# Attention and a feed-forward layer on one core: late weight conversion, sums of x and the hand-over put in other places

## The chip, the core and the metric

The kernel runs on one core of a Trainium2 chip. A core has engines with instruction streams of their own: TensorE (PE, the matrix products, with PEld for its weight loads), VectorE (DVE), ScalarE (ACT), GpSimd (POOL) and SyncE (SP), which here issues nearly all DMAs. Each works through its stream in order and waits on semaphores for the others. The metric is the device time of one execution in microseconds; lower is better.

## The reference

Two layers, the second on the first one's output. `f` gives a decay along the sequence, the weights arrive as 64-bit floats.

```python
B, H, S, D = 8, 8, 576, 64
scores = np.matmul(q, k.transpose(0, 1, 3, 2)) / np.sqrt(D)
cum = np.cumsum(np.log(np.clip(f, 0.0001, 1.0)), axis=-1)
scores = np.where(causal, -1e9, scores + cum[:, :, :, None] - cum[:, :, None, :])
...
x = softmax(scores) @ v                  # laid out as 4608 tokens x 512
h = x @ w_in                             # 512 x 2048
g = h * erf(softplus(h))
return g @ w_out                         # 2048 x 512
```

## The kernel before

**Attention** is a pipeline over t = 0 to 68 with 64 steps of work (NH = 64: 32 pairs of heads, each in two halves). For step t it issues scores(t), the reductions and exponentials, normalize(t-2), transposes(t-3), values(t-4) and store(t-5). `store` copies the outputs o from PSUM into a tile xo on DVE (L564, L567, L568) and writes it to the DRAM tensor xt_d from SP's queue (L570). From t = 64 on, the products of the first two feed-forward units run between the last steps.

**The weights** come as 64-bit floats and are turned on the chip into a high and a low part in float32r (a type that TensorE multiplies in one pass), written to DRAM as wi_d and wo_d. A pair of feature blocks (called a feature here, numbered 0 to 7) has four raw tiles. For each: `words` (three DVE operations, L351 to L353) and `joined` (two, L360 and L369), then for w_out `out_high` on ACT and `out_low` on POOL (L380), for w_in `combine` (sums on POOL, L388), `in_high` on ACT and `in_low` on POOL (L398). `schedule` lays them out as a list of steps; `due` says how many are issued by each t. In the feed-forward part, `middle` takes two more steps in every unit, one between the flushes (after flush 3) and one behind the rounding of the gates.

**The feed-forward part** takes tokens in six blocks v of 768 and features in nine visits: blocks 0 to 2 with features 0 to 4, blocks 0 to 2 with features 5 to 7, blocks 3 to 5 with all eight. A unit is one feature of one visit; there are 48: units 0 to 14 (visits of five), 15 to 23 (visits of three), 24 to 47 (visits of eight). Within a unit, x @ w_in is done in seven products of half blocks, P1 to P7, instead of eight. Their x operands, numbered 0 to 6 in the order of the products, are the blocks 11, 12, 21, 22 of x and the differences T1, T2, "12" (in place of block 12) and T4. Each operand becomes a tile xs with a high part (ACT, L136) and a low part (two POOL operations, L140). The differences (two operations each, L131) are made on DVE, for the first visit alone on POOL. Each of P1 to P7 is six matmuls: high by high, high by low, low by high, for two halves of the depth.

The products go to PSUM banks a, b, x, y; P2 adds to P1 in a, so P2 must wait until DVE has copied P1 (L186). All of a's to y's banks exist once. For unit u, `middle(u)` issues on PE the products with w_out in six groups of six (`down`, L234), on ACT softplus and erf of unit u+1 (L205, L207, with table loads), on DVE six flushes that add y to a sum in SBUF (L253, L255) and four gates (h times erf, L215) between them, then `round_gate`: gh on ACT (L222), gl on POOL (L223); then `prepare`, which takes an equal share of the next visit's `x_steps`. After that come `up(u+2, 0)`, P1, P6, P7, P5 with the copy and three additions on DVE (L182), `up(u+2, 1)`, P2, P4, P3 with two additions, and the load of the weights of unit u+4. y has four buffers, each of u, e, gh, gl six, a weight tile two.

Work is issued by hand in program order for PE, DVE, ACT and POOL; a position in the code is a position in the engine's stream.

## Time and profile before

| | |
|---|---|
| median of 3 runs | 1206.84 us (1206.11 to 1208.26) |
| the profiled execution | 1209.55 us |
| its span, from the first to the last instruction | 1207.7 us |
| granted clock of TensorE, mean | 0.964 |
| share of the span that PE, DVE, ACT, POOL are busy | 92%, 71%, 59%, 51% |
| read and written in HBM | 231.88 MB, 46.81 MB |

A row of the timeline gives start, length, engine, line, operation, output <- inputs, shapes and count; in brackets how long the engine idled ahead of it and what ended that. Equal instructions in a row are put together (x6). In the order listings further down a row is one instruction (x2: two alike), named by line, operation and tiles; a tile's number tells it from others of the name.

In the page's 40 slices the clock (PEclk) and PE's share dip in the same places, the end of attention and the visits after it:

```profile
PE   5999899999995698979999898989999999999998
PEclk7999999999998798989999999989999999999999
```

### The profile page before, as it was taken

How to read it: one execution, taken by the hardware profiler on the slowest of the kernel's cores; microseconds unless marked ns; L12 is line 12 of the kernel's file. 1: busy time of each engine (PE TensorE's matmuls, PEld its weight loads, DVE VectorE, ACT ScalarE, POOL GpSimd, SP SyncE). 2: the span in 40 equal slices, each digit the busy share in tenths (PEclk: the TensorE clock that was granted, in tenths of full speed). 3: DMA queues.
4: the chain of work that ended last, by engine and by line, in shares of the span. 5: the costliest groups of instructions: out<-in, count | busy, mean ns of one | idle time of the engine just before them, and what ended most of it. 6: DMA issues, size and time to landing. Idle time of an engine off the chain costs nothing. (4 is left out here: it accounts for less than half of the span.)

```text
span 1207.7 us, 21855 instructions
## 1 busy us (share of the span) xinstructions
PE 1113.5 (92%) x7552; PEld 971.2 (80%) x7552; DVE 857.3 (71%) x1964; ACT 713.6 (59%) x1540; POOL 619.7 (51%) x734
## 2 busy tenths in 40 slices
PE   5999899999995698979999898989999999999998
PEld 3888788887885587868888877777899989999997
DVE  6888789998985677776766666575766676665555
ACT  3787678887874154536566455454565556555553
POOL 1666657788754346447445554545444434442233
PEclk7999999999998798989999999989999999999999
DMA  8698998878856456937847676747455755566532
GB/s 300 210 316 306 341 340 279 254 272 298 294 192 225 158 180 247 316 120 254 312 157 252 235 257 223 262 182 245 183 192 209 262 183 187 188 204 232 192 131 87
DMA packets 75725, 280.11 MB, mean 232 GB/s; under 512 B 7904, under 2 KB 17120, under 8 KB 63328
## 3 DMA queue, kind: packets, MB, share of 16 engines
q1 hardware_dynamic: 75616, 278.72, 66.2%
q8 instruction: 60, 0.98, 0.3%
q14 instruction: 49, 0.40, 0.1%
HBM read 231.88 MB, written 46.81 MB: 231 GB/s over the span
## 5 line engine op out<-in xcount | busy, mean ns | idle before, releaser
L223 POOL TENSOR_TENSOR gl<-e,gh 128x384 fp32r<-128x384 f32 x192 | 234.5, 1250 | 454.5 <-PE y L234 370.3
L234 PE MATMUL y<-wo,gh 128*128 128x512 f32 x1152 | 357.5, 392 | 13.6 <-DMA wo<-wo_d 13.6
L234 PEld LDWEIGHTS y<-wo,gh 128*128 128x128 f32 x1152 | 217.0, 189 | 57.2 <-issue 13.7
L255 DVE TENSOR_TENSOR ys<-y,ys 128x512 f32<-128x512 f32 x252 | 174.2, 691 | 97.4 <-PE y L234 97.4
L234 PE MATMUL y<-wo,gl 128*128 128x512 f32 x576 | 225.8, 392 | 0.0
L516 POOL TENSOR_SCALAR pr<-pr,st 128x576 f32<-128x576 f32 (+4 forms) x320 | 164.5, 535 | 118.1 <-DVE st L512 74.2
L505 ACT ACTIVATE pr<-pr,st 128x576 f32<-128x576 f32 (+3 forms) x320 | 176.7, 557 | 3.5 <-DVE st L493 3.5
L176 PE MATMUL pha<-xs,wi 128*128 128x384 f32 x576 | 125.3, 352 | 41.4 <-DVE u L186 40.3
L493 DVE CUSTOM_DVE_ANT_0 pr<-s,c 128x576 f32<-128x576 f32 (+3 forms) x320 | 136.4, 487 | 28.7 <-PE s L475 20.8
L176 PEld LDWEIGHTS pha<-xs,wi 128*128 128x128 f32 x576 | 105.3, 195 | 51.3 <-DVE u L186 41.7
L222 ACT CAST gh<-e 128x384 fp32r<-128x384 f32 x192 | 93.9, 514 | 83.8 <-DVE e L215 83.3
L205 ACT ACTIVATE e<-pha 128x384 f32<-128x384 f32 x48 | 23.6, 492 | 191.4 <-PE pha L176 184.1
L470 PE MATMUL s<-k,q 64*128 64x320 f32 (+4 forms) x768 | 121.1, 428 | 14.4 <-DMA k<-in_k_dram 8.3
L176 PE MATMUL phy<-xs,wi 128*128 128x384 f32 x576 | 123.5, 346 | 4.8 <-POOL xs L140 4.7
L234 PEld LDWEIGHTS y<-wo,gl 128*128 128x128 f32 x576 | 108.6, 189 | 22.9
L176 PE MATMUL phx<-xs,wi 128*128 128x384 f32 x576 | 125.0, 352 | 1.1 <-POOL xs L140 1.1
L205 ACT ACTIVATE e<-u 128x384 f32<-128x384 f32 x144 | 75.0, 522 | 77.0 <-DVE u L182 73.9
L182 DVE TENSOR_TENSOR u<-phx,u 128x384 f32<-128x384 f32 x96 | 53.5, 558 | 93.9 <-PE phx L176 91.9
L470 PEld LDWEIGHTS s<-k,q 64*128 64x128 f32 x768 | 80.9, 196 | 45.1 <-issue 20.4
L537 ACT COPY pt<-t 128x512 f32<-128x512 f32 x128 | 73.6, 577 | 71.2 <-PE t L528 71.2
L555 PE MATMUL o<-pt,v 128*64 128x128 f32 (+1 forms) x1920 | 104.4, 262 | 12.2 <-DVE xo L564 6.5
L555 PEld LDWEIGHTS o<-pt,v 128*64 128x64 f32 x1920 | 95.6, 139 | 22.1 <-issue 6.3
(68 smaller groups left out, 1709.8 us busy)
## 6 DMA issues: line engine op xcount, KB each, us to landing
wi<-wi_d SPq DMA_DIRECT2D x48, 1792.0 KB, 7.4
wo<-wo_d SPq DMA_DIRECT2D x48, 1024.0 KB, 4.8
v<-in_vp_dram SPq DMA_DIRECT2D x32, 576.0 KB, 7.2
c<-cum_d SPq DMA_DIRECT2D x62, 288.0 KB, 5.7
r<-xt_d SPq DMA_DIRECT2D x36, 384.0 KB, 4.7
q<-in_q_dram SPq DMA_DIRECT2D x32, 320.0 KB, 5.7
k<-in_k_dram SPq DMA_DIRECT2D x32, 288.0 KB, 6.0
xt_d<-xo SPq DMA_DIRECT2D x32, 288.0 KB, 7.2
```

The source lines that it names most:

```text
L176: nc.tensor.matmul(out=ps, lhsT=wi[:, w, n, kd], rhs=xs[:, x, kd], start=not part and kd == 0 and i == 0, stop=kd == 1 and i == 2, skip_gr ...
L205: nc.scalar.activation(out=e_, in_=h[c], func=AF.Softplus)
L222: nc.scalar.copy(out=gh, in_=e_)
L223: nc.gpsimd.tensor_tensor(out=gl, in0=e_, in1=gh.bitcast(F32), op=ALU.subtract)
L234: nc.tensor.matmul(out=y, lhsT=x[:, cs], rhs=wo[:, i, w], start=i == 0 and n == 0, stop=i == 1 and n == 2)
L255: nc.vector.tensor_tensor(out=ys, in0=y, in1=ys, op=ALU.add)
L470: nc.tensor.matmul(out=s[j][:, at:at + k1 - k0], lhsT=q[h, PAD + START[i]:PAD + END[i]], rhs=k[h, k0:k1], start=i > 0, stop=k1 < END[i])
L493: nc.vector.tensor_tensor_reduce(out=to[:, ::-1] if j else to, in0=score, in1=decay_, scale=-0.125, scalar=BIG, op0=ALU.add, op1=ALU.min, ...
L505: nc.scalar.activation(out=seg, in_=seg, func=AF.Exp, bias=st[:, 0, j, m:m + 1], scale=-1.0, accum_out=st[:, 1, j, m:m + 1])
L516: nc.gpsimd.tensor_scalar(out=seg, in0=seg, scalar1=st[:, 2, j, m:m + 1], scalar2=1.0, op0=ALU.mult, op1=ALU.mult)
L537: nc.scalar.copy(out=pt[:, 512 * a:512 * a + 512], in_=b)
L555: nc.tensor.matmul(out=o[h, to:to + width], lhsT=v[:, ch, h], rhs=pt[:, at[j]:at[j] + width], start=n == 0, stop=n == len(parts) - 1, skip ...
```

## The change

PE's order stays. Five things move:

- Conversion in attention ends with feature 4. The steps of features 5 to 7 get places of their own beside units 0 to 12 (`beside_units`): place 0 is ahead of flush 0 (`words` on DVE; `out_low`, `combine`, `in_low` on POOL), place 1 between the two parts of `up` (`joined`), place 2 behind the rounding (`out_high`, `in_high`).
- The differences of x go to the same places (`combine` of the class): T1 to place 0 of a visit's first unit, T2 and "12" to place 1 of it, T4 to place 0 of the unit after the one with xs 4. For visits 1 to 3 POOL makes them, for visits 4 to 8 DVE.
- `SPLITS` says which operands are split in which unit of the visit ahead.
- At the end of attention, activation and gates of unit 0 come at the end of step 65 instead of its start; the last store of xt_d is issued from ACT's queue; the load of the weights of unit 3 comes behind the first two loads of wo.
- Two tiles share another tag, and ACT's xs tiles 3, 4, 6 of odd visits come from the pool that held 3, 4, 5.

```diff
@@
     RINGS = {"u": 6, "e": 6, "gh": 6, "gl": 6}
     PRODUCTS = [("P1", "a"), ("P6", "b"), ("P7", "x"), ("P5", "y"), ("P2", "a"), ("P4", "x"), ("P3", "y")]
     FIRST = 4
+    X = ["11", "T2", "12", "T1", "21", "T4", "22"]
+    SPLITS = {3: [[0, 3, 4, 6], [1, 2, 5]], 5: [[0, 4], [3, 6], [1, 2], [5]], 8: [[0], [4], [3], [6], [1], [2], [5]]}
     TILES = ["11", "21", "22", "12"]
 
     def __init__(self, tc, xt_d, out, xp, wp):
@@
             self.nc.sync.dma_start(out=r, in_=self.xt_d[2 * i * P:2 * (i + 1) * P, c:c + TB]
                                    .rearrange("(k p) t -> p k t", p=P))
 
+    def sub(self, k, name, kds=range(2)):
+        nc, raw = self.nc, self.raw
+        a, b = {"T1": ("12", "11"), "T2": ("22", "T1"), "12": ("22", "12"), "T4": ("21", "T2")}[name]
+        if name != "12" and (k, name) not in raw:
+            raw[k, name] = self.half(name, k)
+        for kd in kds:
+            (nc.vector if k > HALF else nc.gpsimd).tensor_tensor(
+                out=raw[k, name][:, kd], in0=raw[k, a][:, kd], in1=raw[k, b][:, kd], op=ALU.subtract)
+
+    def high(self, k, n):
+        pool, bufs = (self.xq, 3) if k % 2 and n in (3, 4, 6) else (self.xp, 10)
+        self.xs[k, n] = x = pool.tile([P, 2, 2, TB], F32R, name=f"xs{k}_{n}", tag="xs", bufs=bufs)
+        self.nc.scalar.copy(out=x[:, 0], in_=self.raw[k, self.X[n]])
+
+    def low(self, k, n, kds=range(2)):
+        x = self.xs[k, n]
+        for kd in kds:
+            self.nc.gpsimd.tensor_tensor(out=x[:, 1, kd], in0=self.raw[k, self.X[n]][:, kd],
+                                         in1=x[:, 0, kd].bitcast(F32), op=ALU.subtract)
+
     def x_steps(self, k):
 
...
         steps = []
...
+        for n in range(7):
+            for name in {0: ("T1", "T2", "12"), 5: ("T4",)}.get(n, ()):
+                steps += [(self.sub, k, name, [kd]) for kd in range(2)]
+            steps += [(self.high, k, n)] + [(self.low, k, n, [kd]) for kd in range(2)]
         return steps
 
     def load_wi(self, u):
@@
             row = v * NW + tb * P
             nc.sync.dma_start(out=self.out[row:row + P] if a == NU - 1 else self.part_d[v * NTB + tb], in_=ys)
 
+    def combine(self, u, between):
+
+        k, i, a = self.units[u]
+        if k + 1 < len(self.visits):
+            four = [4 in n for n in self.SPLITS[len(self.visits[k][1])]].index(True) + 1
+            names = ("T2", "12") if between else ("T1",)
+            for name in names if i == 0 else ("T4",) if i == four and not between else ():
+                self.sub(k + 1, name)
+
     def prepare(self, u):
 
         k, i, a = self.units[u]
-        n = len(self.visits[k][1])
-        if i == 0:
-            self.later = self.x_steps(k + 1)
-        if i < n - 1:
-            for _ in range(-(-len(self.later) // (n - 1 - i))):
-                self.later.pop(0)()
-        if i == n - 2:
-            self.load_x(k + 2)
+        splits = self.SPLITS[len(self.visits[k][1])]
+        if k + 1 < len(self.visits) and i < len(splits):
+            for n in splits[i]:
+                self.high(k + 1, n)
+                self.low(k + 1, n)
+            if i == len(splits) - 1:
+                self.load_x(k + 2)
 
     def middle(self, u, convert):
 
         more = u + 1 < self.n
         ys = [self.down(u, tb) for tb in range(NTB)]
+        convert(u, 0)
+        self.combine(u, False)
         if more:
             self.activate(u + 1)
-        order = [("f", 0), ("f", 1), ("g", 0), ("f", 2), ("g", 1), ("f", 3), ("c", 0), ("g", 2), ("f", 4), ("g", 3),
-                 ("f", 5)]
+        order = [("f", 0), ("f", 1), ("g", 0), ("f", 2), ("g", 1), ("f", 3), ("g", 2), ("f", 4), ("g", 3), ("f", 5)]
         for what, n in order:
             if what == "f":
                 self.flush(u, n, ys[n])
-            elif what == "c":
-                convert()
             elif more:
                 self.gate(u + 1, n)
         if more:
             for n in range(4):
                 self.round_gate(u + 1, n)
-            convert()
+            convert(u, 2)
             self.prepare(u)
         del self.wo[u], self.g[u]
         self.load_wo(u + 2)
@@
                 work[8 * b + n].append((call, a, *args))
         return [work[n] for n in range(8 * len(features) + 5)]
 
+    def convert(steps):
...
@@
                 nc.vector.tensor_copy(out=xo[:, 192:448], in_=o[:, :256])
                 nc.vector.tensor_copy(out=xo[:, :64], in_=o[:, 256:320])
                 b, pp = divmod(p, NP)
-                nc.sync.dma_start(out=xt_d[pp * P:(pp + 1) * P, b * S:(b + 1) * S], in_=xo)
+                queue = nc.sync if t < NH - 1 else nc.scalar
+                queue.dma_start(out=xt_d[pp * P:(pp + 1) * P, b * S:(b + 1) * S], in_=xo)
                 del vals[p]
 
         NH = B * H
 
-        fd = [wk.tile([P, S], F32, name=f"fd{j}", tag=f"pt{j}", bufs=1) for j in range(2)]
+        fd = [wk.tile([P, S], F32, name=f"fd{j}", tag=f"pr{j}") for j in range(2)]
         for j in range(2):
             nc.sync.dma_start(out=fd[j], in_=f[0, j].partition_broadcast(P))
         fr = wk.tile([B * H, S], F32, name="fr", tag="xo")
@@
         load(1)
         load_weight(0)
         load_weight(1)
-        work = schedule(range(NU))
+        work = schedule(range(NU1 + 1))[:8 * NU1 + 5]
+        work[-1] = [step for step in work[-1] if step[0] is in_low]
         for t in range(NH + 5):
             there = [0 <= t - n < NH for n in range(6)]
             p, half = divmod(t, 2)
@@
                 moe.up((t - NH) // 2, (t - NH) % 2)
                 if t == NH + 1:
                     moe.load_wi(2)
-                    moe.activate(0)
-                    for n in range(4):
-                        moe.gate(0, n)
-                        moe.round_gate(0, n)
-                if t == NH + 3:
-                    moe.load_wi(3)
             if there[2]:
                 normalize(t - 2)
             if there[5]:
@@
             if there[3]:
                 for a in range(1, len(BANKS[(t - 3) % 2])):
                     evacuate(t - 3, a)
-            due = 2 * t + 2 if t < 4 else 8 + (8 * NU1 - 3) * (t - 3) // (NH - 4) if t < NH else 8 * NU1 + 6 + t - NH
-            while 8 * NU + 5 - len(work) < due:
-                convert(work)
+            due = 2 * t + 2 if t < 4 else 8 + (8 * NU1 - 4) * (t - 3) // (NH - 4)
+            while work and 8 * NU1 + 5 - len(work) < due:
+                convert(work.pop(0))
             if t > X0 and moe.later:
-                moe.later.pop(0)()
+                convert([moe.later.pop(0)])
+            if t == NH + 1:
+                moe.activate(0)
+                for n in range(4):
+                    moe.gate(0, n)
+                    moe.round_gate(0, n)
             if t == NH - 1:
                 early.close()
                 moe.ep = moe_pools.enter_context(tc.tile_pool(name="ep", bufs=2, side="right"))
                 moe.ps_h = moe_pools.enter_context(tc.tile_pool(name="ps_h", bufs=1, space=PSUM, side="right"))
-        assert not moe.later and not pts and not held and not vals
+        assert not work and not moe.later and not pts and not held and not vals
 
     moe.wop = ctx.enter_context(tc.tile_pool(name="wop", bufs=1))
     moe.xq = ctx.enter_context(tc.tile_pool(name="xq", bufs=1))
@@
     moe.ps_y = ctx.enter_context(tc.tile_pool(name="ps_y", bufs=1, space=PSUM))
     moe.load_wo(0)
     moe.load_wo(1)
+    moe.load_wi(3)
     moe.load_x(1)
     moe.want_y(0)
+    work = beside_units()
     for u in range(moe.n):
-        moe.middle(u, lambda: convert(work))
+        moe.middle(u, lambda u, place: convert(work.pop((u, place), ())))
         if u + 2 < moe.n:
             moe.up(u + 2, 0)
+            convert(work.pop((u, 1), ()))
+            moe.combine(u, True)
             moe.up(u + 2, 1)
             moe.load_wi(u + 4)
     assert not work
```

How the streams change at three places. First, DVE between the flushes of unit 0 and those of unit 1, before (rT and r are the halves of x that the next visit needs, phX the banks, wtop a weight under conversion, ys the sums of y):

```order
L360 SCALAR_TENSOR_TENSOR wtop_5652<-wraw_5494,wtop_5652 128x512
L369 SCALAR_TENSOR_TENSOR wtop_5652<-wraw_5494,wtop_5652 128x512
L131 TENSOR_TENSOR rT_1_5686<-r_1_5576,r_1_5574 128x384 x2
L131 TENSOR_TENSOR rT_1_5689<-r_1_5578,rT_1_5686 128x384 x2
L131 TENSOR_TENSOR r_1_5576<-r_1_5578,r_1_5576 128x384 x2
L186 COPY u_2_5727<-pha_5699 128x384
L182 TENSOR_TENSOR u_2_5727<-phb_5706,u_2_5727 128x384
L182 TENSOR_TENSOR u_2_5728<-phx_5713,u_2_5727 128x384
L182 TENSOR_TENSOR u_2_5728<-phy_5720,u_2_5728 128x384
L182 TENSOR_TENSOR u_2_5733<-phx_5713,u_2_5727 128x384
L182 TENSOR_TENSOR u_2_5727<-phy_5720,u_2_5727 128x384
L255 TENSOR_TENSOR ys_0_5582<-y_0_5756,ys_0_5582 128x512
```

The same place after the change, from the first addition behind the copy of P1 on:

```order
L181 TENSOR_TENSOR u_2_5680<-phb_5659,u_2_5680 128x384
L181 TENSOR_TENSOR u_2_5681<-phx_5666,u_2_5680 128x384
L181 TENSOR_TENSOR u_2_5681<-phy_5673,u_2_5681 128x384
L366 SCALAR_TENSOR_TENSOR wtop_5591<-wraw_4959,wtop_5591 128x512
L375 SCALAR_TENSOR_TENSOR wa_5688<-wraw_4959,wtop_5591 128x2x256
L181 TENSOR_TENSOR u_2_5686<-phx_5666,u_2_5680 128x384
L181 TENSOR_TENSOR u_2_5680<-phy_5673,u_2_5680 128x384
L357 TENSOR_SCALAR wtop_5761<-wraw_5194 128x512
L358 TENSOR_SCALAR wtop_5761<-wtop_5761 128x512
L359 TENSOR_SCALAR wtop_5761<-wtop_5761 128x512
L254 TENSOR_TENSOR ys_0_5543<-y_0_5719,ys_0_5543 128x512
```

The six differences are gone from ahead of the copy (L186 before); the pair L366, L375 of `joined` stands between the additions of the two parts, and the three of `words` ahead of flush 0 (L254).

Second, DVE at the end of attention, before, from the last additions of unit 1's products to the first flush (xo is the tile for the last store):

```order
L182 TENSOR_TENSOR u_1_5451<-phx_5431,u_1_5445 128x384
L182 TENSOR_TENSOR u_1_5445<-phy_5438,u_1_5445 128x384
L564 COPY xo_5518<-o_5474 128x2x128
L351 TENSOR_SCALAR wtop_5540<-wraw_5413 128x512
L352 TENSOR_SCALAR wtop_5540<-wtop_5540 128x512
L353 TENSOR_SCALAR wtop_5540<-wtop_5540 128x512
L567 COPY xo_5518<-o_5520 128x256
L568 COPY xo_5518<-o_5520 128x64
L360 SCALAR_TENSOR_TENSOR wtop_5540<-wraw_5413,wtop_5540 128x512
L369 SCALAR_TENSOR_TENSOR wtop_5540<-wraw_5413,wtop_5540 128x512
L253 COPY ys_0_5582<-y_0_5588 128x512
```

and after:

```order
L181 TENSOR_TENSOR u_1_5431<-phx_5411,u_1_5425 128x384
L181 TENSOR_TENSOR u_1_5425<-phy_5418,u_1_5425 128x384
L585 COPY xo_5492<-o_5454 128x2x128
L588 COPY xo_5492<-o_5494 128x256
L589 COPY xo_5492<-o_5494 128x64
L357 TENSOR_SCALAR wtop_5591<-wraw_4959 128x512
L358 TENSOR_SCALAR wtop_5591<-wtop_5591 128x512
L359 TENSOR_SCALAR wtop_5591<-wtop_5591 128x512
L252 COPY ys_0_5543<-y_0_5549 128x512
```

The words and joined steps no longer stand between and behind the copies of xo; one weight's words come behind them.

Third, POOL in units 15 and 16, the first visit of three units (gl are the low parts of the gates of a unit; xs the operands of the next visit), before:

```order
L140 TENSOR_TENSOR xs_0_8075<-r_4_7761,xs_0_8075 128x384 x2
L140 TENSOR_TENSOR xs_1_8079<-rT_4_8070,xs_1_8079 128x384 x2
L140 TENSOR_TENSOR xs_2_8083<-r_4_7763,xs_2_8083 128x384 x2
L223 TENSOR_TENSOR gl_11_8212<-e_11_8188,gh_11_8211 128x384
L223 TENSOR_TENSOR gl_21_8216<-e_21_8192,gh_21_8215 128x384
L223 TENSOR_TENSOR gl_22_8220<-e_22_8190,gh_22_8219 128x384
L223 TENSOR_TENSOR gl_12_8224<-e_12_8194,gh_12_8223 128x384
L140 TENSOR_TENSOR xs_3_8227<-rT_4_8067,xs_3_8227 128x384 x2
L140 TENSOR_TENSOR xs_4_8231<-r_4_7767,xs_4_8231 128x384 x2
L140 TENSOR_TENSOR xs_5_8238<-rT_4_8235,xs_5_8238 128x384 x2
L140 TENSOR_TENSOR xs_6_8242<-r_4_7765,xs_6_8242 128x384 x2
```

and after:

```order
L140 TENSOR_TENSOR xs_0_8070<-r_4_7761,xs_0_8070 128x384 x2
L140 TENSOR_TENSOR xs_3_8074<-rT_4_8028,xs_3_8074 128x384 x2
L140 TENSOR_TENSOR xs_4_8078<-r_4_7767,xs_4_8078 128x384 x2
L140 TENSOR_TENSOR xs_6_8082<-r_4_7765,xs_6_8082 128x384 x2
L222 TENSOR_TENSOR gl_11_8219<-e_11_8195,gh_11_8218 128x384
L222 TENSOR_TENSOR gl_21_8223<-e_21_8199,gh_21_8222 128x384
L222 TENSOR_TENSOR gl_22_8227<-e_22_8197,gh_22_8226 128x384
L222 TENSOR_TENSOR gl_12_8231<-e_12_8201,gh_12_8230 128x384
L140 TENSOR_TENSOR xs_1_8234<-rT_4_8123,xs_1_8234 128x384 x2
L140 TENSOR_TENSOR xs_2_8238<-r_4_7763,xs_2_8238 128x384 x2
L140 TENSOR_TENSOR xs_5_8242<-rT_4_8192,xs_5_8242 128x384 x2
```

Unit 15 has four operands (0, 3, 4, 6) instead of three, and unit 16 the three that are left, with operand 1, which P6 takes second.

More of the change, by code (lines that the diff above doesn't have):

```diff
@@ L119, in load_x @@
                                    .rearrange("(k p) t -> p k t", p=P))
-    def x_steps(self, k):
-        if k >= len(self.visits):
-            return []
-        nc, raw = self.nc, self.raw
-        engine = nc.vector if k else nc.gpsimd
-        def sub(name, a, b, kd):
-            if kd == 0 and name != "12":
-                raw[k, name] = self.half(name, k)
-            engine.tensor_tensor(out=raw[k, name][:, kd], in0=raw[k, a][:, kd], in1=raw[k, b][:, kd], op=ALU.subtract)
-        def high(n, nm):
-            pool, bufs = (self.xq, 3) if k % 2 and 2 < n < 6 else (self.xp, 10)
-            self.xs[k, n] = x = pool.tile([P, 2, 2, TB], F32R, name=f"xs{k}_{n}", tag="xs", bufs=bufs)
-            nc.scalar.copy(out=x[:, 0], in_=raw[k, nm])
-        def low(n, nm, kd):
-            x = self.xs[k, n]
-            nc.gpsimd.tensor_tensor(out=x[:, 1, kd], in0=raw[k, nm][:, kd], in1=x[:, 0, kd].bitcast(F32),
-                                    op=ALU.subtract)
-        steps = []
-        for name, a, b in (("T1", "12", "11"), ("T2", "22", "T1"), ("12", "22", "12")):
-            steps += [lambda args=(name, a, b, kd): sub(*args) for kd in range(2)]
-        for n, nm in enumerate(("11", "T2", "12", "T1", "21", "T4", "22")):
-            if n == 5:
-                steps += [lambda args=("T4", "21", "T2", kd): sub(*args) for kd in range(2)]
-            steps.append(lambda n=n, nm=nm: high(n, nm))
-            steps += [lambda args=(n, nm, kd): low(*args) for kd in range(2)]
@@ L416, in schedule, with beside_units @@
         return [work[n] for n in range(8 * len(features) + 5)]
-    def convert(work):
-        for call, *args in work.pop(0) if work else ():
+    def beside_units():
+        work = defaultdict(list)
+        for b, a in enumerate(range(NU1, NU)):
+            b, out0, out1, in0, in1 = 4 * b - 2, 4 * a, 4 * a + 1, 4 * a + 2, 4 * a + 3
+            for at, place, call, *args in (
+                    (b, 0, words, out0), (b, 1, joined, out0), (b + 1, 0, words, out1), (b + 1, 1, joined, out1),
+                    (b + 1, 2, out_high, a, 0), (b + 2, 0, words, in0), (b + 2, 0, out_low, a, 0), (b + 2, 1, joined, in0),
+                    (b + 2, 2, out_high, a, 1), (b + 3, 0, words, in1), (b + 3, 0, out_low, a, 1), (b + 3, 1, joined, in1),
+                    (b + 4, 0, combine, a, 3, 2, 1, 6), (b + 4, 2, in_high, a, 0, 4), (b + 5, 0, in_low, a, (0, 2), (2, 4)),
+                    (b + 5, 2, in_high, a, 4, 7), (b + 6, 0, in_low, a, (4, 6), (6, 7))):
+                if at >= 0:
+                    work[at, place].append((call, *args))
+        return work
+    def convert(steps):
+        for call, *args in steps:
             call(*args)
```

## The prediction

> **What bounds the kernel now.** I read the page's head and busy table first, then the table by windows, then the waits, then the timeline around each wait.
>
> ```profile
> span 1207.7 us, 21855 instructions
> PE 1113.5 (92%) x7552; PEld 971.2 (80%) x7552; DVE 857.3 (71%) x1964; ACT 713.6 (59%) x1540; POOL 619.7 (51%) x734
> ```
>
> TensorE (PE) is busy for 92% of the span; what can be won without fewer products is the rest, and the time in which its products run slow. The profiled execution took 1209.55 us, 1.85 more than its span; the sum is made against that span. The median of the runs, 1206.84, lies 2.7 below that execution, and the gain is taken from it unscaled.
>
> The chain of waits shows what an undisturbed unit takes (start, length, what):
>
> ```profile
> 860.23 8.20 PE y L234 x36
> ...
> 875.74 8.20 PE y L234 x36
> ...
> 1187.49 16.44 PE y L234 x72
> ```
>
> From one start of the products with w_out to the next is 15.51 us, and PE alone fills it. The windows split the feed-forward part at the starts of units 0, 7, 15 and 24, up to the end of PE's work (columns: window, its length, busy PE, PEld, DVE, ACT, POOL, PE's clock, DMA share, GB/s):
>
> ```profile
> 396.22:542.52 146.30, 122.05 (x547) 107.17 (x547) 109.98 (x160) 64.50 (x107) 71.71 (x62) 0.90 0.57 201
> 542.52:671.65 129.13, 126.74 (x626) 113.88 (x626) 81.51 (x138) 76.06 (x126) 68.99 (x63) 0.99 0.70 250
> 671.65:842.95 171.30, 152.72 (x704) 130.79 (x704) 109.51 (x168) 90.60 (x148) 89.77 (x78) 0.96 0.66 229
> 842.95:1203.93 360.98, 358.89 (x1789) 322.56 (x1788) 227.69 (x384) 199.23 (x334) 136.88 (x120) 1.00 0.53 188
> ```
>
> Beyond 15.51 a unit there are: in units 0 to 6, 146.30 - 108.57 = 37.7; units 7 to 14, 129.13 - 124.08 = 5.0; units 15 to 23, 171.30 - 139.59 = 31.7; after that, 360.98 - 22 x 15.51 - 16.44 = 3.3. Together 77.7 us, and the clock column (0.90, 0.96) says that part of it is slow products. The waits name the cause (total, times, longest):
>
> ```profile
> PE pha L176 <- DVE u L186: 40.3, 13, 7.3
> PE y L234 <- DMA wo<-wo_d: 13.6, 1, 13.6
> ```
>
> P2 adds into the bank that P1 filled, so it waits until VectorE (DVE) has copied P1 (L186). The copy of unit 2 is late, in unit 0:
>
> ```profile
> 410.29 1.40 DVE L369 SCALAR_TENSOR_TENSOR wtop<-wraw,wtop 128x512 int32<-128x512 int32 x1
> 411.61 2.88 DVE L131 TENSOR_TENSOR rT<-r,r 128x384 f32<-128x384 f32 x2
> ...
> 417.87 0.55 DVE L186 COPY u<-pha 128x384 f32<-128x384 f32 x1
> ...
> 418.47 2.29 PE L176 MATMUL pha<-xs,wi 128*128 128x384 f32 x6 [7.33 <-DVE u L186]
> ```
>
> A conversion step and, from 411.61 to 417.87, six sums of x stand ahead of the copy in DVE's order. The wait costs twice, since PE comes back slow: six products take 2.29 where 15.51 - 8.20 over 42 makes 1.04. In unit 1 the words of a weight stand there, and unit 5's wait is short:
>
> ```profile
> 434.37 0.65 DVE L351 TENSOR_SCALAR wtop<-wraw 128x512 int32<-128x512 int32 x1
> 435.05 1.12 DVE L352 TENSOR_SCALAR wtop<-wtop 128x512 f32<-128x512 f32 x1
> 436.20 1.10 DVE L353 TENSOR_SCALAR wtop<-wtop 128x512 int32<-128x512 int32 x1
> ```
> ```profile
> 437.82 1.56 PE L176 MATMUL pha<-xs,wi 128*128 128x384 f32 x6 [2.11 <-DVE u L186]
> 439.19 2.25 PE L176 MATMUL phx<-xs,wi 128*128 128x384 f32 x6
> ...
> 497.14 1.31 PE L176 MATMUL pha<-xs,wi 128*128 128x384 f32 x6 [1.49 <-DVE u L186]
> ```
>
> So a wait of 2.1 us costs about 2 more in slow products (0.5 + 1.2 in these two rows, and the third group), one of 1.5 some 0.3 in its row. The Trainium skill, "TensorE: Matmul & The Clock Gate", section "What's actually happening", has the half rate come after a window of about 3.4 us of idling. The trace has it after 2.11; by the page, waits of 2 us that are left over would cost half of what the rows say.
>
> **The change, part by part.** *Units 0 to 6.* The steps leave the place ahead of the copy for two others: ahead of flush 0, and between the two parts of the up products. An undisturbed unit, which starts at 906.59, has this room on DVE:
>
> ```profile
> 908.18 0.69 DVE L255 TENSOR_TENSOR ys<-y,ys 128x512 f32<-128x512 f32 x1 [0.83 <-PE y L234]
> ...
> 916.06 0.56 DVE L186 COPY u<-pha 128x384 f32<-128x384 f32 x1 [0.37 <-PE pha L176]
> ...
> 921.26 0.56 DVE L182 TENSOR_TENSOR u<-phx,u 128x384 f32<-128x384 f32 x1 [1.52 <-PE phx L176]
> ```
>
> It idles 0.83 ahead of flush 0 and 1.52 between the parts. y has four buffers, so the fifth of the six groups waits only if flush 0 ends later than 4 x 8.20 / 6 = 5.5 into the unit; here it ends at 2.3. Three words last 2.9 by the rows of unit 1, two joined steps 2.8 by 410.29. At these slow prices: adds of part 0 end 13.2 into the unit, joined 2.8, two adds 1.1, words 2.9, flush 0.7: 20.7, which is 5.2 into the next unit, just inside. Queued behind the words are the flushes, the gates and the copy, all some 3 later; the copy ends then near 12.5 and P2 is due at 8.20 + 4.16 = 12.4. I keep 2.4 of slow products in unit 0, where PE starts slow after an idle stretch (396.22 below: two products in 1.19, of which 36 take 8.20), about 0.3 a unit for late flushes and 1 where xs 5 comes last: 5 left of 37.7, **gain 33** (28 to 35). Sums for the early targets go to POOL:
>
> ```profile
> 516.21 1.02 DVE L131 TENSOR_TENSOR rT<-r,r 128x384 f32<-128x384 f32 x2
> ```
> ```profile
> L131 POOL TENSOR_TENSOR rT<-r,r 128x384 f32<-128x384 f32 x2 | 2.2, 1094 | 0.0
> ```
>
> One is 0.51 on DVE undisturbed, 1.1 on POOL. POOL is busy for 71.71 of 146.30, so eight of them a visit are covered by its idling unless they hold up gl.
>
> *Units 7 to 14.* The sums of x in unit 10, the same stall as in unit 0, go to POOL: **gain 3.6** of 5.0 (0 to 5).
>
> *Units 15 to 23, visits of three units.* Here the sums stay on DVE, beside POOL:
>
> ```profile
> 739.03 2.64 DVE L131 TENSOR_TENSOR rT<-r,rT 128x384 f32<-128x384 f32 x2
> ```
> ```profile
> 739.95 2.59 POOL L140 TENSOR_TENSOR xs<-r,xs 128x384 fp32r<-128x384 f32 x2
> ...
> 913.00 4.61 POOL L223 TENSOR_TENSOR gl<-e,gh 128x384 fp32r<-128x384 f32 x4 [7.98 <-PE y L234]
> ```
>
> Each is 1.3 there. The waits of the copy go, but the first unit now issues eight lows (xs 0, 3, 4, 6) behind its gl: from 11.0 into the unit they take 8 to 10 us. T2 and "12" run beside them, 4 x 1.3 from 13.2 to 18.4; two adds to 19.5; T4, 2.6, to 6.6 of the next unit; flush 0 to 7.3, 1.8 past its limit. Gates and gl slip, gl to about 14.5, and behind gl stands xs 1. P6 of the next visit wants it at 9.3 + 1.8 = 11.1 and gets it at 16.5: 5 us of waiting and some 1.5 of slow products, 8.3 a visit with the flush. Three visits: 25 left of 31.7, **gain 6.6**. Ends: 31 if the lows stay ahead of PE, -5 if gl of the third unit slips too; I take a value near the low end, as the row of 739.03 has DVE at its slow price in this stage.
>
> *Units 24 to 47.* Two copies behind sums (1.6 each) get a place with 0.83 + 1.52 of idling: **gain 3.2** (0 to 3.3).
>
> *The hand-over.* The wait of 13.6, and PE, DVE and SP ahead of it:
>
> ```profile
> 365.00 3.04 PE L555 MATMUL o<-pt,v 128*64 128x128 f32 x32 [4.42 <-DVE xo L564]
> ...
> 396.22 1.19 PE L234 MATMUL y<-wo,gh 128*128 128x512 f32 x2 [13.63 <-DMA wo<-wo_d]
> ```
> ```profile
> 380.70 1.38 DVE L351 TENSOR_SCALAR wtop<-wraw 128x512 int32<-128x512 int32 x1
> ...
> 384.20 0.21 DVE L568 COPY xo<-o 128x64 f32<-128x64 f32 x1
> ```
> ```profile
> 380.81 0.38 SPq L156 DMA_DIRECT2D wi<-wi_d  x1
> 384.45 0.32 SPq L570 DMA_DIRECT2D xt_d<-xo  x1
> ...
> 390.26 0.80 SPq L162 DMA_DIRECT2D wo<-wo_d  x2
> ```
>
> wo waits for the last store of xt_d in both orders (5.8 from 384.45 to 390.26), then lands at 396.2, 5.9 later. The wait of 4.42 goes, as the copy of o no longer stands behind the gates; but the gates now come later, and P1 of unit 1 waits for the first of them, since it reads the bank that P1 overwrites: some 4.0, so only about 1.6 is won there. The words go from between the last copies (another 1.2), so the store is issued near 381.6. It moves past SP's queue to ACT's, with the softplus of unit 1 behind it; wi 3 (1792 KB) moves from ahead of it to behind wo. At the old 5.8 + 5.9 PE starts at 393.4; with each 3 shorter, at 387.5. I take 390: **gain 6** (3 to 8.5). Attention before that issues a step less: 0.5 (0 to 1).
>
> **Sum**: 33 + 3.6 + 6.6 + 3.2 + 6 + 0.5 = 53; 1207.7 - 53 = 1155 of span, 1206.84 - 53 = **1154** in the median of the runs. Its own range: the ends of units 0 to 14 and of the hand-over lie 12 below and 6 above their terms if all come at once; I take 8 either way, 1146 to 1162. The ends of units 15 to 23 are rivals.
>
> **The rivals.** *A, a new wait: flush 0.* If POOL holds DVE up at both new places in units 1 to 9, DVE has 0.3 us to spare there (5.5 - 5.2). For it speaks the word of 380.70, 1.38 long, which runs beside this:
>
> ```profile
> 380.51 2.70 POOL L398 TENSOR_TENSOR wa<-wa,whi 128x512 f32<-128x512 f32 x2 [0.41 <-ACT whi L392]
> ```
>
> The change issues such POOL steps just ahead of the words. Against it stands that POOL idles for half of these units. Four waits of 2 with 2 of slow products are 16 us: **1170**. The Trainium skill, "SBUF — State Buffer", section "SBUF: two separate sides", makes the port that both share an exclusive lock, held for a whole instruction. By that rule each word waits for the end of POOL's current step; the two rows bear it out here, as the words last about as long as POOL's 1.35.
>
> *B, the three-unit visits come out clean,* because gl and xs 1 keep ahead: 12 to 16 more, **1140**. For it: POOL is busy only 89.77 of 171.30. Against: it comes in one piece behind gl.
>
> *C, the change doesn't do what it says at the hand-over:* wo is held by something else and PE starts at 396 as before: **1160**.
>
> *D, slower.* The one place that could do it is flush 0 of every unit 0 to 14. The other terms win 16, so the 42.7 of excess there would have to become 59, 3.9 a unit: a wait of 2 and 2 of slow products in each of the fifteen, which needs flush 0 at 7.5 and DVE held up 2.3 longer than its slow prices. From then on it is above **1207**. Units 10 to 14 have no conversion on DVE, which speaks against it.
>
> **How the numbers follow.** My forecast 0.45, A 0.22, B 0.20, C 0.08, no net change 0.02, D 0.03. Range 1138 to 1178: B's and A's values with 2 and 8 us for the unknown costs, where A reaches six such units. Faster by over 0.2% (2.4 us, about what can be told apart here) 0.95, within it 0.02, slower 0.03.
>
> **What would show it.** Right: the wait of PE on L186's copy under 5 us in all; windows of units 0 to 6 near 114 with a clock of 0.97 or more; PE's wait on wo near 10 with its start near 390; a wait of PE on xs of about 5 in three units of 15 to 23. Wrong: waits of PE for y's buffer (A), units 15 to 23 near 142 (B), or the wait on wo as long as before (C).

## The result and the profile after

The changed kernel took 1151.49 us in the median of 4 runs (1148.79 to 1155.79) against 1206.72 for the kernel before (4 runs): a ratio of 0.9544, 95% interval 0.9513 to 0.9575. That is 55.2 us; forecast were 53 and a median of 1154. The profiled execution was the longest of the four (1155.79, with a span of 1154.0; the other spans were 1147.0, 1150.2 and 1149.2), so its parts are compared with a forecast span of 1155.

The page of the changed kernel, its head, its busy line, and two lines of the 40 slices:

```profile
span 1154.0 us, 21827 instructions
...
PE 1097.6 (95%) x7552; PEld 964.3 (84%) x7552; DVE 839.1 (73%) x1940; ACT 711.5 (62%) x1540; POOL 634.9 (55%) x758
...
PE   5999899999998599999999898989999999999998
...
PEclk9999999999999899999999998989999999999999
```

The dips after the end of attention are gone but for three near the middle. The table by windows, split at the starts of the same units 0, 7, 15, 24 and the end of PE's work (columns as in the prediction):

```profile
390.35:502.93 112.58, 111.92 (x546) 99.91 (x547) 97.66 (x142) 65.07 (x107) 86.06 (x76) 0.98 0.70 259
502.93:628.46 125.53, 124.92 (x626) 112.32 (x625) 93.85 (x145) 77.10 (x128) 84.80 (x78) 1.00 0.78 285
628.46:792.52 164.06, 150.34 (x703) 133.28 (x703) 106.50 (x168) 89.31 (x148) 84.69 (x78) 0.94 0.68 240
792.52:1150.20 357.68, 357.68 (x1789) 322.69 (x1788) 222.80 (x384) 198.81 (x334) 133.35 (x120) 1.00 0.53 189
```

Excess is the length beyond 15.51 us a unit.

| stage | excess before | forecast to be left | left |
|---|---|---|---|
| units 0 to 6 | 37.7 | 5 | 112.58 - 7 x 15.51 = 4.0 |
| units 7 to 14 | 5.0 | 1.4 | 125.53 - 8 x 15.51 = 1.4 |
| units 15 to 23 | 31.7 | 25 | 164.06 - 9 x 15.51 = 24.5 |
| units 24 to 47 | 3.3 | 0.1 | 357.68 - 22 x 15.51 - 16.44 = 0.0 |
| start of unit 0 | 396.22 | 390 | 390.35 |

Of the waits of PE, that on the copy of P1 (40.3 us before) is gone from the list; these are the largest left in the feed-forward part (total, times, longest):

```profile
PE y L233 <- issue: 10.7, 1, 10.7
...
PE phb L175 <- ACT xs L135: 6.4, 3, 2.2
PE phb L175 <- POOL xs L140: 5.9, 3, 2.0
...
PE y L233 <- DVE ys L254: 2.0, 4, 0.5
```

The first is the wait for wo, though "issue" says that the profile shows no releaser. The second and third come once in each of the three visits of three units, and the last is the y buffer of rival A, nearly closed.

### The profile page after: what moved, and what is told of

It reads as the page before. It is cut to its first block, busy times and chain, and to the rows that moved or that the text cites. A ratio compares the mean times of both kernels' runs of the same rounds, so it can differ in the third digit from the quotient of the medians.

```text
span 1154.0 us, 21827 instructions
## 1 busy us (share of the span) xinstructions
PE 1097.6 (95%) x7552; PEld 964.3 (84%) x7552; DVE 839.1 (73%) x1940; ACT 711.5 (62%) x1540; POOL 634.9 (55%) x758
## 4 chain that ended last, share of the span: by engine, by line
PE 55%; DVE 4%; POOL 1%; issue 1%; ACT 0%; POOLq 0%; DVEq 0%; ACTq 0%
PE y L233 28%; PE phy L175 8%; PE phx L175 8%; PE pha L175 7%; PE phb L175 4%; DVE rT L129 1%; DVE ys L254 1%; DVE e L214 1%; DVE r L129 1%; POOL gl L222 0%; POOL xs L140 0%; DVE u L181 0%; ACT gh L221 0%; ACT L206 0%; ACT e L206 0%
## 5 line engine op out<-in xcount | busy, mean ns | idle before, releaser
L222 POOL TENSOR_TENSOR gl<-e,gh 128x384 fp32r<-128x384 f32 x192 | 219.6, 1175 | 379.6 <-PE y L233 323.1
L254 DVE TENSOR_TENSOR ys<-y,ys 128x512 f32<-128x512 f32 x252 | 172.5, 688 | 69.6 <-PE y L233 69.6
L175 PE MATMUL pha<-xs,wi 128*128 128x384 f32 x576 | 118.7, 341 | 4.2 <-DVE e L214 4.1
L175 PE MATMUL phx<-xs,wi 128*128 128x384 f32 x576 | 118.7, 341 | 0.6 <-POOL xs L140 0.6
L175 PE MATMUL phy<-xs,wi 128*128 128x384 f32 x576 | 118.0, 340 | 0.0
L576 PEld LDWEIGHTS o<-pt,v 128*64 128x64 f32 x1920 | 95.1, 138 | 17.3 <-issue 5.4
```

What stands on the lines that cost most here:

```text
L175: nc.tensor.matmul(out=ps, lhsT=wi[:, w, n, kd], rhs=xs[:, x, kd], start=not part and kd == 0 and i == 0, stop=kd == 1 and i == 2, skip_gr ...
L222: nc.gpsimd.tensor_tensor(out=gl, in0=e_, in1=gh.bitcast(F32), op=ALU.subtract)
L254: nc.vector.tensor_tensor(out=ys, in0=y, in1=ys, op=ALU.add)
L576: nc.tensor.matmul(out=o[h, to:to + width], lhsT=v[:, ch, h], rhs=pt[:, at[j]:at[j] + width], start=n == 0, stop=n == len(parts) - 1, skip ...
```

## The experiments

All ratios are to the kernel before, run on the same chip. Where two kernels' intervals overlap (sums_on_dve or wi3_late and the change, early and in_order, store_apart and early), the medians alone don't tell them apart, and the reading rests on windows and waits of the traces.

| kernel | median us | ratio, 95% interval |
|---|---|---|
| handover_alone | 1207.25 | 0.9988 (0.9974 to 1.0002) |
| x_as_before | 1182.05 | 0.9793 (0.9767 to 0.9820) |
| words_twice | 1166.28 | 0.9641 (0.9615 to 0.9667) |
| sums_on_dve | 1155.54 | 0.9569 (0.9547 to 0.9592) |
| the change | 1151.49 | 0.9544 (0.9513 to 0.9575) |
| store_on_sp | 1150.16 | 0.9534 (0.9502 to 0.9567) |
| wi3_late | 1147.57 | 0.9497 (0.9478 to 0.9517) |
| t2_ahead | 1144.07 | 0.9459 (0.9437 to 0.9481) |
| in_order | 1134.23 | 0.9384 (0.9357 to 0.9411) |
| early | 1129.15 | 0.9335 (0.9306 to 0.9364) |
| store_apart | 1125.65 | 0.9315 (0.9292 to 0.9338) |
| best | 1117.65 | 0.9254 (0.9235 to 0.9273) |

### One part alone, or undone: conversion, sums, hand-over

**handover_alone.** The kernel before, with this alone:

```diff
                moe.later.pop(0)()
+            if t == NH + 1:
+                moe.activate(0)
+                for n in range(4):
+                    moe.gate(0, n)
+                    moe.round_gate(0, n)
...
+                queue = nc.sync if t < NH - 1 else nc.scalar
...
     moe.load_wo(1)
+    moe.load_wi(3)
```

> The kernel before with the hand-over of the change alone (gates of unit 0 later, last store from ACT's queue, unit 3's weights asked for behind wo); conversion and sums stay. My theory: the words still stand between the last copies of o, so only the wait for the gates is won: the products with w_out start near 394.6 instead of 396.2, gain 1 to 2 us (about 1205). Rival, the queue of the store is what counts: they start near 391, gain 5 to 6 (about 1201).

Its median is 1.6 us lower, with an interval that just holds no change. DVE and PE in its timeline:

```profile
380.49 0.42 DVE L351 TENSOR_SCALAR wtop<-wraw 128x512 int32<-128x512 int32 x1
...
382.41 0.42 DVE L567 COPY xo<-o 128x256 f32<-128x256 f32 x1 [0.59 <-PE o L555]
382.76 0.21 DVE L568 COPY xo<-o 128x64 f32<-128x64 f32 x1
```
```profile
367.34 1.39 PE L176 MATMUL pha<-xs,wi 128*128 128x384 f32 x6 [4.11 <-DVE e L215]
...
394.38 1.19 PE L234 MATMUL y<-wo,gh 128*128 128x512 f32 x2 [12.01 <-DMA wo<-wo_d]
```

The wait for the first gate is there (4.11), and unit 0 starts at 394.38 (394.6 expected). But the reason given was wrong: the words still stand between the copies, yet they are short here (0.42 for the first, 1.38 before), and DVE idles 0.59 behind them for PE's last products. So the words no longer delay the store, and the last copy ends 0.6 behind those products, as in the change. What is left of the wait of 12.01 is the store, 5.2 until wo is asked for at 388.19, and wo, 6.2 until it lands. That conversion stood in the way of this reordering is not shown.

**x_as_before.** The changed kernel with the sums and splits of x where they were, the sums all on DVE again:

```diff
-            (nc.vector if k > HALF else nc.gpsimd).tensor_tensor(
+            (nc.vector if k else nc.gpsimd).tensor_tensor(
...
         convert(u, 0)
-        self.combine(u, False)
...
-            for n in splits[i]:
-                self.high(k + 1, n)
-                self.low(k + 1, n)
+            for _ in range(-(-len(self.later) // (n - 1 - i))):
+                call, *args = self.later.pop(0)
+                call(*args)
...
             convert(work.pop((u, 1), ()))
-            moe.combine(u, True)
```

> The changed kernel with sums and splits of x as before (on DVE, ahead of the copy of P1, in even shares), conversion and hand-over as changed. My theory: each visit's first unit waits for the copy again, 4.4 us in units 0, 5 and 10, the visits of three units go back from 24.5 to about 31.7, units 24 and 32 lose 1.6 each: 13 + 7 + 3 = 23 slower, about 1175; conversion is then worth some 24 of the 55. Rival, conversion alone made the waits and the sums fit beside it: 1152 to 1158.

30.6 us slower than the change, more than the 23 expected. Its waits:

```profile
PE pha L177 <- DVE u L187: 23.2, 8, 4.4
```

The wait on the copy is back in the first unit of eight visits, as expected; visits of three units went to 33.4 us of excess (31.7 expected), units 0 to 14 to 24.6. There my sum counted only the first unit of each visit, but units 3, 8 and 9 lost 2.9, 3.5 and 1.4 as well (1.5, 0 and 0 in the change), probably to shares of `x_steps` beside conversion; no run isolates that. By the ratios, some 25 of the change's 55 us come with conversion and hand-over while the sums are in their old place, and some 30 with sums and splits on top. The expected 1175 had put it the other way round, at 32 and 23.

**sums_on_dve.**

```diff
-            (nc.vector if k > HALF else nc.gpsimd).tensor_tensor(
+            (nc.vector if k else nc.gpsimd).tensor_tensor(
```

> The changed kernel with the sums of x of visits 1 to 3 on DVE, at the same places. My theory: joined and four sums stand ahead of the last two additions in units 0 and 5, words ahead of flush 0 after that, so flush 0 of units 1 and 6 ends 3 to 4 us past its limit: 8 to 14 us slower (1160 to 1165), all of it in units 0 to 7. Rival, POOL against DVE makes no difference at these places: 1150 to 1153.

The median is 4.0 higher where 8 to 14 were expected: right in place, too high in size. The excess of units 0 to 6 is 7.7 against 4.0 (1.3 in unit 1, 2.5 in unit 6); four kernels that share the change's code there (store_on_sp, t2_ahead, in_order, early) have 4.0 to 4.4. In units 7 to 14 about 1 is left, no more than in the change, so there it is the new place of the sums that counts and not the engine. Its wait for y, and DVE in unit 0:

```profile
PE y L233 <- DVE ys L254: 5.0, 6, 2.2
```
```profile
407.16 2.11 DVE L129 TENSOR_TENSOR rT<-r,rT 128x384 f32<-128x384 f32 x2
409.19 1.01 DVE L129 TENSOR_TENSOR r<-r,r 128x384 f32<-128x384 f32 x2
```

The four sums took 3.1, where I had put them all at the slow price of 1.3 each; only the first two were slow.

**words_twice.** Each `words` at place 0 is followed by the same three operations once more (`again`), which write the same values.

```diff
...
-                    work[at, place].append((call, *args))
+                    work[at, place] += [(call, *args)] + ([(again, *args)] if call is words else [])
```

> The changed kernel with the three word operations of features 5 to 7 done twice at their place ahead of flush 0 (the second pass writes the same values); units 0 to 9 but for those without words. It prices the slack behind the limit of flush 0, 5.5 us into the unit. In the changed kernel the words last 1.3 to 3.9 and flush 0 ends 3 to 5.6 into the unit. My theory (PE waits for the fifth y buffer from 5.5 on, with 2 us of slow products from 2 us of waiting): 2 to 4 us in most of ten units, 15 to 30 slower, 1166 to 1182, and all of it in units 1 to 9. Rival, the flushes have more slack than that and only the copy of P1 counts: under 5 slower.

14.8 slower, 1166.28 where 1166 to 1182 were expected: at the low end. The wait for y's buffer went from 2.0 to this:

```profile
PE y L233 <- DVE ys L254: 11.9, 8, 3.0
```
```profile
414.44 1.22 PE L233 MATMUL y<-wo,gh 128*128 128x512 f32 x2 [3.01 <-DVE ys L254]
```

It stands 5.7 into unit 1, ahead of the fifth group, and behind it two products take 1.22, like those at 396.22 in the kernel before. The losses are 6.0 in unit 1, then 2.5, 3.1, 2.0 and 3.9 in units 3, 6, 7 and 8, fewer units than expected. Nor does each wait cost double, as units 6 and 8 show:

```profile
500.15 0.74 PE L233 MATMUL y<-wo,gh 128*128 128x512 f32 x2 [2.73 <-DVE ys L254]
...
535.50 0.73 PE L233 MATMUL y<-wo,gh 128*128 128x512 f32 x2 [2.00 <-DVE ys L254]
```

The granted clock of the 6 us behind the wait of 2.73 is 1.00; behind the wait of 2.00 it is 0.72, and behind that of 3.01 in unit 1 it is 0.52. So rival A's mechanism is real, with its limit where it was put, but its price of 2 us of slow products for 2 us of waiting holds for some waits only. In the change flush 0 comes right up to the limit, as its unit 3 shows (start 439.21, limit 444.7):

```profile
440.27 1.09 DVE L357 TENSOR_SCALAR wtop<-wraw 128x512 int32<-128x512 int32 x1
441.39 1.40 DVE L358 TENSOR_SCALAR wtop<-wtop 128x512 f32<-128x512 f32 x1
442.82 1.41 DVE L359 TENSOR_SCALAR wtop<-wtop 128x512 int32<-128x512 int32 x1
444.16 1.27 DVE L254 TENSOR_TENSOR ys<-y,ys 128x512 f32<-128x512 f32 x2
```

### The visits of three units

In the changed kernel, DVE, POOL and PE in units 15 (from 628.46) and 16 (from 643.97):

```profile
641.52 2.60 DVE L129 TENSOR_TENSOR rT<-r,rT 128x384 f32<-128x384 f32 x2
644.04 2.66 DVE L129 TENSOR_TENSOR r<-r,r 128x384 f32<-128x384 f32 x2
646.62 0.55 DVE L181 TENSOR_TENSOR u<-phx,u 128x384 f32<-128x384 f32 x1
...
649.35 1.28 DVE L254 TENSOR_TENSOR ys<-y,ys 128x512 f32<-128x512 f32 x2
```
```profile
643.66 4.89 POOL L140 TENSOR_TENSOR xs<-r,xs 128x384 fp32r<-128x384 f32 x4
653.48 4.20 POOL L222 TENSOR_TENSOR gl<-e,gh 128x384 fp32r<-128x384 f32 x4 [4.94 <-PE y L233]
```
```profile
656.29 0.44 PE L175 MATMUL phb<-xs,wi 128*128 128x384 f32 x1 [2.13 <-ACT xs L135]
658.68 1.97 PE L175 MATMUL phb<-xs,wi 128*128 128x384 f32 x5 [1.96 <-POOL xs L140]
660.45 2.12 PE L175 MATMUL phx<-xs,wi 128*128 128x384 f32 x6
```

T2 and "12" (the first two DVE rows) take 5.3 beside POOL's lows and hold up the additions; softplus, gates and gl follow, and xs 1 stands behind gl. But POOL idles 4.94 ahead of gl: it isn't short of time. Three kernels tell the two readings apart, too much work for POOL or work in the wrong order.

**t2_ahead.**

```diff
-            names = ("T2", "12") if between else ("T1",)
+            three = len(self.visits[k][1]) == 3
+            names = () if three and between else ("T1", "T2", "12") if three else ("T2", "12") if between else ("T1",)
```

> The changed kernel; in the visits of three units T2 and "12" stand beside T1 ahead of flush 0 of the first unit, while POOL idles, and no longer between the two parts of the up products. My theory (DVE beside POOL delays additions, softplus, gates and gl, and xs 1 stands behind gl): gl of the second unit runs from 6.4 to 11 into the unit, xs 1 is ready at 13.0 where P6 wants it at 9.3; 3.7 of waiting and 2 of slow products instead of 8.2 a visit: about 1144. Rival, POOL's eight lows are too many for one unit whatever DVE does: 8.2 a visit stay, 1150 to 1152.

**in_order**, from t2_ahead; T4 keeps its place in the second unit (`four`):

```diff
-    SPLITS = {3: [[0, 3, 4, 6], [1, 2, 5]], 5: [[0, 4], [3, 6], [1, 2], [5]], 8: [[0], [4], [3], [6], [1], [2], [5]]}
+    SPLITS = {3: [[0, 1, 2, 3], [4, 5, 6]], 5: [[0, 4], [3, 6], [1, 2], [5]], 8: [[0], [4], [3], [6], [1], [2], [5]]}
...
-            four = [4 in n for n in self.SPLITS[len(self.visits[k][1])]].index(True) + 1
+            four = 1 if len(self.visits[k][1]) == 3 else [4 in n for n in self.SPLITS[len(self.visits[k][1])]].index(True) + 1
```

> As t2_ahead, and the visits of three units split operands 0, 1, 2, 3 in the first unit and 4, 5, 6 in the second, in the order in which the products take them. My theory (what counts is which operand stands behind the second unit's gl): P6 doesn't wait; P2, P4 and P3 wait 0.6 to 1.1 each for xs 4, 5 and 6, 3 to 5 us a visit with slow products: 1136 to 1142. Rival, POOL's amount of work: as t2_ahead or worse, above 1144.

**early**, from t2_ahead, with in_order's line for `four`:

```diff
-    SPLITS = {3: [[0, 3, 4, 6], [1, 2, 5]], 5: [[0, 4], [3, 6], [1, 2], [5]], 8: [[0], [4], [3], [6], [1], [2], [5]]}
+    SPLITS = {3: [[3, 1, 2, 6], [5]], 5: [[0, 4], [3, 6], [1, 2], [5]], 8: [[0], [4], [3], [6], [1], [2], [5]]}
...
                 self.load_x(k + 2)
+        if i == len(self.visits[k][1]) - 1 and k + 1 < len(self.visits) and len(self.visits[k + 1][1]) == 3:
+            for n in (0, 4):
+                self.high(k + 2, n)
+                self.low(k + 2, n)
```

> As t2_ahead, and operands 0 and 4 of the visit after the next are split one unit earlier, in the last unit of the visit before, which had no such work; then 3, 1, 2, 6 and 5. My theory: POOL is through with the lows 4 us into the second unit, T4 and gl are on time, xs 5 is ready at 13.1 where P4 wants it at 13.4: 0 to 1.5 a visit, 1128 to 1133. Rival, the halves of x land too late for the earlier split, or T4 beside the lows delays flush 0: 3 or more a visit, above 1137.

They came out 7.4, 17.3 and 22.3 us ahead of the change: t2_ahead and early as expected, in_order at 1134.23 better than its range of 1136 to 1142, with 1.8 left a visit where 3 to 5 were expected. The window of units 15 to 23, in t2_ahead, in_order and early:

```profile
628.85:781.22 152.37, 145.88 (x704) 129.50 (x704) 98.61 (x168) 89.97 (x148) 83.92 (x78) 0.97 0.73 258
```
```profile
624.93:769.99 145.06, 142.91 (x703) 125.84 (x703) 98.62 (x168) 89.97 (x148) 84.11 (x78) 1.00 0.77 272
```
```profile
623.36:762.92 139.56, 139.56 (x704) 126.57 (x703) 98.65 (x168) 88.49 (x146) 80.36 (x74) 1.00 0.79 283
```

POOL's busy time is nearly the same in the first two (84.69 in the change; early moves four of its operations out of this window), DVE's falls by 8 as the sums leave POOL's side, and the excess falls from 24.5 over 12.8 and 5.5 to 0.0. (Four other kernels that share the change's code in these units have 21.7 to 24.1.) So the stall was order, not work: first the sums beside the lows, then an operand that is wanted second and made behind gl. In t2_ahead gl and the wait that is left:

```profile
650.77 4.59 POOL L222 TENSOR_TENSOR gl<-e,gh 128x384 fp32r<-128x384 f32 x4 [2.49 <-PE y L233]
```
```profile
656.37 1.97 PE L175 MATMUL phb<-xs,wi 128*128 128x384 f32 x5 [1.98 <-POOL xs L140]
```

gl began at 6.4 into the unit, which started at 644.36, as expected; the wait was 1.98 rather than 3.7, as P6's first matmul needs only the high part and its second only half of the low, which POOL had 1 us before the whole.

### The hand-over

PE, DVE, ACT and SP of the changed kernel around the last store:

```profile
364.61 2.29 PE L175 MATMUL pha<-xs,wi 128*128 128x384 f32 x6 [4.10 <-DVE e L214]
...
390.35 1.19 PE L233 MATMUL y<-wo,gh 128*128 128x512 f32 x2 [10.72 <-issue]
```
```profile
380.00 0.21 DVE L589 COPY xo<-o 128x64 f32<-128x64 f32 x1
```
```profile
380.25 0.35 ACTq L592 DMA_DIRECT2D xt_d<-xo  x1
```
```profile
376.92 0.32 SPq L155 DMA_DIRECT2D wi<-wi_d  x1
385.39 0.80 SPq L161 DMA_DIRECT2D wo<-wo_d  x2
```

The store is issued right behind the copy, wo follows 5.14 later and lands 4.96 after that. The weights of unit 3 are asked for at 376.92, ahead of both, though the code has them behind wo.

**store_on_sp.**

```diff
-                queue = nc.sync if t < NH - 1 else nc.scalar
+                queue = nc.sync
```

> The changed kernel with the last store of xt_d issued from SP again. My theory: SP has issued unit 3's weights at 376.9 and is free when the copy ends at 380.2, so the queue doesn't matter: 1151.5 within 1 us, start of the products with w_out near 390.3. Rival, the other queue lets the store pass the weights: 2 to 3 us slower, start near 393.

No difference: 1150.16, and PE waits 10.73 for wo, as long as in the change. Its start, 387.93, is earlier only because attention ended 2.4 earlier in that execution (see the end). The queue makes no difference here.

**wi3_late.** Without `moe.load_wi(3)` ahead of the loop, the same load is issued in `middle(0)` from ACT's queue, behind softplus and erf of unit 1.

```diff
-    moe.load_wi(3)
...
             self.activate(u + 1)
+            if u == 0:
+                self.load_wi(3, self.nc.scalar)
```

> The changed kernel with the load of unit 3's weights issued from ACT's queue behind softplus and erf of unit 1, so that it really comes behind the load of wo (in the changed kernel SP issues it 8 us ahead of wo, not behind it as my prediction had it). My theory: the last store then lands in about 3 us instead of 5.0 and wo in 4 to 5; PE's wait ahead of unit 0 falls from 10.7 to 7.5 to 9, 2 to 3 us faster: about 1149. Rival, this load is no burden for the other two: 10.7 stays, 1150.5 to 1152.5.

```profile
376.13 0.35 ACTq L594 DMA_DIRECT2D xt_d<-xo  x1
```
```profile
383.57 1.19 PE L233 MATMUL y<-wo,gh 128*128 128x512 f32 x2 [8.07 <-DMA wo<-wo_d]
```

wo is asked for at 378.39 here, so the store took 2.3 instead of 5.1, and wo 5.2, about as long as in the change. The wait falls by 2.65 (the median by 3.9, but the intervals overlap). The load was a burden for the store.

**store_apart**, on early: the last xo from the pool of conversion (`cv`, tag "whi") instead of `wk`.

```diff
-                held["x"] = xo = wk.tile([P, S], F32, name=f"xo{p}", tag="xo")
+                pool, tag, bufs = (wk, "xo", 2) if p < NH // 2 - 1 else (cv, "whi", 1)
+                held["x"] = xo = pool.tile([P, S], F32, name=f"xo{p}", tag=tag, bufs=bufs)
```

> As early, and the tile xo of the last pair of heads lies in the pool of the weight conversion instead of attention's own, so that the first load of wo needn't wait until the last store of xt_d has landed, only for the last products and copies of attention. My theory (that landing is what PE waits for at the hand-over, about 5 us): wo is asked for near 379.7 instead of 385.4, competes with unit 3's weights, and the products with w_out start 3.5 to 5 us earlier than in early: 1124 to 1126. Rival, the load is held up by the other traffic: within 1.5 of early, 1128 to 1130.

```profile
373.90 0.32 SPq L155 DMA_DIRECT2D wi<-wi_d  x1
376.69 0.81 SPq L161 DMA_DIRECT2D wo<-wo_d  x2
```
```profile
384.67 1.19 PE L233 MATMUL y<-wo,gh 128*128 128x512 f32 x2 [8.07 <-DMA xt_d<-xo]
```

wo no longer waits for the store: it is asked for at 376.69, ahead of the store at 377.22. But it takes 8.0 to land beside unit 3's weights, so the wait falls by 2.6 from 10.62 in early, where 3.5 to 5 were expected (the median falls by 3.5, with overlapping intervals). The row names the store, but it is wo that PE waits for: in best PE starts at 377.36 with the store, issued at 372.30 and 7.7 in landing, still under way.

**best** is store_apart with the late load of wi3_late, and issues softplus and erf of unit 0 at the start of step 65 again.

```diff
                     moe.load_wi(2)
+                    moe.activate(0)
...
             if t == NH + 1:
-                moe.activate(0)
                 for n in range(4):
```

> As store_apart; softplus and erf of unit 0 are issued at the start of step 65 again (the gates stay at its end), and the load of unit 3's weights is issued from ACT's queue behind softplus and erf of unit 1, out of the way of wo. My theory: P1 of unit 1 waits 1.5 less for the first gate, wo lands 1 to 2 sooner: 1121 to 1124. Rival, the copies of pt behind erf hold up attention's last products by as much, and wo's time isn't set by the other load: 1124 to 1126 like store_apart.

```profile
span 1115.3 us, 21838 instructions
...
PE 1082.9 (97%) x7552; PEld 955.1 (86%) x7552; DVE 827.8 (74%) x1940; ACT 712.2 (64%) x1540; POOL 635.7 (57%) x758
```
```profile
358.21 1.31 PE L175 MATMUL pha<-xs,wi 128*128 128x384 f32 x6 [0.63 <-DVE e L214]
...
377.36 1.19 PE L233 MATMUL y<-wo,gh 128*128 128x512 f32 x2 [5.68 <-DMA wo<-wo_d]
```

1117.65, better than both theories' ranges. The wait for the first gate fell from 4.10 to 0.63, by 3.5 where 1.5 was expected, as the copies of pt no longer stand ahead of softplus. The products behind it no longer come back slow: P1, P6, P7 and P5 together take 4.3 instead of 7.0. And the wait for wo fell from 8.07 to 5.68, with wo landing in 5.6. It beats both kernels: 7.5% less than before (interval 7.3 to 7.7), 33.8 us less than the change.

## Why the prediction was right, point by point

- **The copy of P1.** Confirmed: its wait of 40.3 us is gone, and x_as_before brings 23.2 of it back. The excess of units 0 to 6 fell by 33.7 (33), of units 7 to 14 by 3.6 (3.6), though POOL was not needed for the latter (sums_on_dve).
- **The new places hold the work, barely.** Slow prices gave an end of flush 0 at 5.2 of 5.5 us. In unit 3 its row puts the end at about 5.6 (half of 1.27 behind 444.16, less 439.21), a little past the limit; the waits for y total 2.0 us, and words_twice opens this wait. The places of loss were right too: 2.3 in unit 0 (2.4 forecast), 1.5 in unit 3, the one where xs 5 comes last.
- **Visits of three units.** 24.5 instead of 25, 8.2 a visit. That it is so close is luck in part: pieces of the term were off against each other. Flush 0 cost 0.8 (1.8 forecast), waiting for xs 1 4.1 (5), half of it for its high part on ACT, which I had left out, and slow products the remaining 3.3 (1.5). The chain itself is shown by t2_ahead, in_order and early. I had a chance of 0.2 for no stall there; it took another order to get it.
- **Hand-over.** Unit 0 starts 5.9 earlier, where the sum has 6 and 0.5 for attention ahead of it; one step of that sum was wrong, and part of the agreement is luck. Of the 5.9, 1.1 lie ahead of the first up products of unit 0 (347.81 against 346.75), which says little, since early, with the same code there as the change, starts them at 342.31. From there to the last products it is 1.9 (1.6 forecast for the gates). The other 2.9 are the wait for wo: 1.2 since the words no longer hold up the last copy, as forecast, and 1.7 since store and wo land sooner, where 390 needed 3.4. So the hand-over's own share is 4.8, inside 3 to 8.5. The wrong step: I let unit 3's weights move "from ahead of it to behind wo" because the code does. SP's order is not the code's, and the load stayed 3.3 us ahead of the store. Its going shortened the wait by 2.65 in wi3_late. That ACT's queue helps is refuted; the forecast drew nothing from it but the order.
- **Units 24 to 47.** 0.0 left, 0.1 forecast.
- **What the parts are worth singly** was not forecast, and their sizes can't be added: hand-over alone is not told from nothing, conversion with it is worth 25, the sums and splits 30 on top.
- **Rivals.** A is a real limit that the change just about keeps, and its price of 4 us a wait was too high: in words_twice, of the waits of 3.01, 2.73, 1.72 and 2.00, only the first and the last were followed by slow products. B's clean visits need what early does; C and D didn't come.

## What to carry to other kernels

Where TensorE is the bound, list what stands ahead of the one operation it waits for on the other engine, and for each place that is free give the limit by which the next user must be served; a place then holds so much at the slow prices of the rows, and no more. An operand's place in the queue of its maker should follow the order in which the products take it, and nothing that is wanted a unit later (gl here) should stand ahead of it. Where DMAs end a stage, look at the order in which they are really issued, and at what else lands at that time: a load that is wanted much later can hold up the one that is waited for (2.65 us here).

## What the runs showed of the hardware

What a wait of TensorE costs beyond itself varies. Behind the wait for the first gate, 4.11 us in handover_alone and 4.10 in the change, P1's products took 1.39 and 2.29, but the four groups P1, P6, P7 and P5 together took 5.84 and 5.80, so the slow products only came a group later in the one. An undisturbed stretch of the four takes 4.16. Over all kernels with this wait they took from 5.59 (wi3_late) to 7.01 us (store_apart): the same wait cost 1.4 to 2.9 more. Among waits of 2 to 3 us, one of 2.00 was followed by slow products and one of 2.73 was not (words_twice, above); no run shows what decides it.

Attention took a different time in each execution of the same code: its last products began at 377.96 in the change, at 373.52 in early and at 375.54 in store_on_sp, which share that code; a difference of up to 4 us in the start of unit 0 says nothing of the hand-over, only the wait ahead of it does.
